# A decode kernel's key ring grows from 96 to 112 KB a partition, and neighbouring key loads share a quarter of it instead of a half

## The chip, the core and the metric

The kernel runs on one core of one Trainium2 chip. The metric is the device time of one execution in microseconds (us); the runs of the kernel before lie between 1264.14 and 1264.46 us, with a median of 1264.3. The engines are named as in the profile: PE (TensorE, with its weight loads as PEld), DVE (VectorE), ACT (ScalarE), POOL (GpSimd), SP (SyncE, which here issues nearly all DMAs). Keys and values are streamed once from HBM into SBUF, whose 128 partitions are written by 16 DMA engines.

## What is computed

One token attends to a cache of 65,536 keys and values for each of 8 key heads; two query heads share a key head. The result goes through an output projection and is mixed by a gate with a small token MLP, which is little work beside the cache.

```
B, Sq, D = 1, 1, 448
Hq, Hkv, Sk, Dh = 16, 8, 65536, 256

q = (x @ wq)                                   # 16 query heads of 256
k = jnp.repeat(k_cache, rep, axis=1)           # rep = 2
v = jnp.repeat(v_cache, rep, axis=1)
scores = jnp.einsum("bhqd,bhkd->bhqk", q, k) * (Dh ** -0.5)
p = _softmax(scores, axis=-1)
o = jnp.einsum("bhqk,bhkd->bhqd", p, v)
a = o.reshape(B, Sq, Hq * Dh) @ wo
g = _sigmoid((x * gate_w).sum(-1, keepdims=True))
return g * a + (1 - g) * b                     # b: the token MLP
```

The caches are bf16: 8 x 65,536 x 256 x 2 bytes are 268 MB each for keys and for values.

## The kernel before

**Blocks and chunks.** A *block* is 16,384 keys of one head (8 MB of keys, 8 MB of values; four blocks a head, `NP` = 32 blocks in all, numbered j = 0 to 31). Kj and Vj below are the key and the value load of block j. A partition holds 128 rows (`NV`) of 256 numbers of a block, 64 KB. A block is worked off in 8 *chunks* (`BODY`) of 16 rows (`NT`); half a block is 4 chunks (`DC`) or 64 rows (`HV`).

**The work of a block.** For each chunk PE transposes the keys (16 transposes of 128x128, L359; a pair of bf16 numbers is moved as one f32) into the four PSUM banks of `kst`; DVE (L675) and ACT (L820) copy two banks each into `ktT`, and PE multiplies them with the query (L380, 32 small matmuls), one chunk behind the transposes. After the 8 chunks DVE and PE find the running maximum (`maxima`), ACT forms the exponentials of the block (`weights`, L807, into `pT`), DVE fades the old sums, and PE adds the value products (`values`, L411, 128 matmuls). From the fourth block on the order in PE's loop is lagged: iteration j has `maxima` of block j-1, the chunks of block j, and then the values of block j-1.

**Buffers.** Values have one buffer, `vbuf`, of 64 KB a partition: Vj can be loaded when the values of block j-1 are used up (`sem_pv`). Keys have a ring, `kring`, of 192 rows or 96 KB. An even block lies in rows 0 to 127, an odd one in rows 64 to 191, so that neighbours share rows 64 to 127. Each block begins with the shared half: the chunks 0 to 3 read the ring from row 64 (`tiles(HV)`), the chunks 4 to 7 from row 0 or 128 by the parity of the block (`x2`). When a block's first 4 chunks are transposed the next block can be loaded whole. For even blocks the chunks therefore stand in another order than the rows of V, and ACT writes the two halves of the exponentials exchanged into `pT` (`pt_reg` toggles between 0 and `DC`).

**The order of the loads.** SP runs through one list, and each entry waits there until its buffer is free; nothing behind it is issued before. The list is K0 (in halves), V0, K1, V1, K2, K3, V2, K4, V3, K5, V4 and so on. The start differs from the rest: `LEAD` = 2 has K2 and K3 follow each other, K2 comes in two halves (the upper one, which is used first, with its own semaphore), and K3 in a half and two quarters, as the ring comes free; POOL waits for the two quarters and passes them on as one count of `sem_k`. The last key block comes in two halves, and the last value block in five pieces, the first of which (72 rows) goes into the key ring.

PE waits for `sem_k` before chunk 0 of each block, and before chunk 4 for `sem_kb` and, in blocks 2, 3 and 31 alone, for one of `sem_kc`.

Of the kernel before, what the change touches and what calls it, by code (L numbers as in the profile page):

```python
# [12 lines left out]
def bass_gated_mix__gqa_block_cached__mixer_token_mlp__decode_kernel(  # L13
# [14 lines left out]
    bf16 = mybir.dt.bfloat16  # L28
# [35 lines left out]
    LEAD = 2  # L64
# [18 lines left out]


    HV = NV // 2
    assert NP % 2 == 0


# [8 lines left out]
    with ctx:  # L97
        def sb(shape, dt, name):
            return ctx.enter_context(nc.sbuf_tensor(name, shape, dt))
# [4 lines left out]
        def new_sem(name):  # L104
            return ctx.enter_context(nc.semaphore(name))

        kring = sb([P, NV + HV, DH], bf16, "kring")
        kring_f = kring.bitcast(f32)
        vbuf = sb([P, NV, DH], bf16, "vbuf")
        vbuf_f = vbuf.bitcast(f32)  # L110
# [1 line left out]
        pT = sb([P, BODY, 2 * NT], bf16, "pT")  # L112
# [4 lines left out]
        ident = sb([P, P], f32, "ident")  # L117
# [72 lines left out]
        scores_all = sps[:, 0, 0:SC]  # L190
# [6 lines left out]

        sem_k = new_sem("sem_k")
        sem_kb = new_sem("sem_kb")
        sem_kc = [new_sem("sem_kc%d" % i) for i in range(3)]  # L200
        sem_kq = [new_sem("sem_kq%d" % i) for i in range(2)]
        sem_v = new_sem("sem_v")
        sem_vp = [new_sem("semvp%d" % i) for i in range(len(pieces))]
        sem_x = new_sem("sem_x")
# [5 lines left out]
        sem_tr = [new_sem("sem_tr%d" % b) for b in range(NB)]  # L210
# [46 lines left out]
        @block.sync  # L257
        def _(eng):
            def load_wo(g):
                w = A_wo[g * REP * DH:(g + 1) * REP * DH, :]  # L260
                eng.dma_start(wo_rows, w.rearrange("(p i) n -> p (i n)", i=2 * REP)).then_inc(sem_wo, 16)

            load_wo(0)
            eng.dma_start(wq_a.rearrange("p j n -> p (j n)"),
                          A_wq[0:WF * P, :].rearrange("(p j) n -> p (j n)", p=P)).then_inc(sem_wq, 16)
            eng.dma_start(wq_b, A_wq[WF * P:DM, :].rearrange("r (a n) -> (r a) n", a=2)
                          ).then_inc(sem_wq, 16)
            def load(dst, cache, j, n0, n1, at, sem):
                eng.dma_start(dst[:, at + n0:at + n1, :].rearrange("p n d -> p (n d)"), src(cache, j, n0, n1)
                              ).then_inc(sem, 16)  # L270

            load(kring, A_k_cache, 0, HV, NV, 0, sem_k)
            load(kring, A_k_cache, 0, 0, HV, 0, sem_kb)

            def load_v(j):
                if j == 0:
                    eng.wait_ge(s_q, 1)
                    eng.wait_ge(s_hb, 1)
                else:
                    eng.wait_ge(sem_pv, j)  # L280
                load(vbuf, A_v_cache, j, 0, NV, 0, sem_v)
                g, m = divmod(j, PPH)
                if m == 0 and 1 <= g < H - 1:
                    eng.wait_ge(s_proj, g)
                    load_wo(g)

            for j in range(NP):
                if j == LEAD + 1:
                    eng.wait_ge(sem_tr[NB - 1], BODY * LEAD)
                    load(kring, A_k_cache, j, HV, NV, HV, sem_kc[1])  # L290
                    eng.wait_ge(sem_tr[NB - 1], BODY * LEAD + DC // 2)
                    load(kring, A_k_cache, j, 0, HV // 2, HV, sem_kq[0])
                if j >= 1:
                    eng.wait_ge(sem_tr[NB - 1], BODY * (j - 1) + DC)
                if j == LEAD:
                    load(kring, A_k_cache, j, HV, NV, 0, sem_k)
                    load(kring, A_k_cache, j, 0, HV, 0, sem_kc[0])
                elif j == LEAD + 1:
                    load(kring, A_k_cache, j, HV // 2, HV, HV, sem_kq[1])
                elif j == NP - 1:  # L300
                    load(kring, A_k_cache, j, 0, HV, HV, sem_k)
                    load(kring, A_k_cache, j, HV, NV, HV, sem_kc[2])
                elif j >= 1:
                    load(kring, A_k_cache, j, 0, NV, HV * (j % 2), sem_k)
                if j < LEAD:
                    load_v(j)
                elif j > LEAD:
                    load_v(j - 1)


            for (n0, n1), sem in zip(pieces, sem_vp):
                if n0 == 0:
                    eng.wait_ge(sem_tr[NB - 1], BODY * (NP - 1) + DC)
                elif n0 == NRING:
                    eng.wait_ge(sem_pv, NP - 1)
                load(kring if n1 <= NRING else vbuf, A_v_cache, NP - 1, n0, n1, 0, sem)
            eng.wait_ge(s_proj, H - 1)
            for h in range(REP):
                w = A_wo[(HQ - REP + h) * DH:(HQ - REP + h + 1) * DH, :]
                eng.dma_start(wo_sb[:, h, :], w.rearrange("(p j) n -> p (j n)", j=2)).then_inc(sem_wl[h], 16)  # L320
            eng.wait_ge(s_fin, NCG)
            eng.dma_start(out_ap, out_row[:, :]).then_inc(sem_out, 16)
            eng.wait_ge(sem_out, 16)

        @block.gpsimd
        def _(eng):
            eng.memset(ident[:, :], 0.0)
            eng.drain()
            eng.affine_select(
                out=ident[:, :], in_=ident[:, :], compare_op=ALU.not_equal, fill=1.0,  # L330
                base=0, pattern=[[-1, P]], channel_multiplier=1,
            )
            eng.drain()
            eng.memset(ones_sq[:, :], 1.0).then_inc(sem_ident, 1)
            for sem in sem_kq:
                eng.wait_ge(sem, 16)
            eng.sem_inc(sem_k, 16)

        @block.tensor
        def _(pe):  # L340
# [3 lines left out]
            def transposes(k, c, j, u16, x2):  # L344
                if k == 0:
                    pe.wait_ge(sem_k, u16)
                if k == DC:
                    pe.wait_ge(sem_kb, 16)
                    for p, sem in zip((LEAD, LEAD + 1, NP - 1), sem_kc):
                        with pe.If(j == p):  # L350
                            pe.wait_ge(sem, 16)

                done = pe.snap(c + 1, min_val=1, max_val=NC)

                def tiles(at):
                    for b in range(NB):
                        pe.wait_ge(sem_ev[b], done)
                        for i in range(4):
                            ins = pe.transpose(kst[:, b, i * P:(i + 1) * P],  # L359
                                               kring_f[:, at + NT * (k % DC) + 4 * b + i, :], ident[:, :])  # L360
                        ins.then_inc(sem_tr[b], 1)

                if k < DC:
                    tiles(HV)
                else:
                    with pe.If(x2 == 0):
                        tiles(0)
                    with pe.Else():
                        tiles(NV)

            def scores(k, c, j1):
                par = k % 2
# [165 lines left out]
            with nc.Fori(0, NP + 1, 1, engines=on, head_slot={pe.engine: 0}) as jj:  # L538
                j = pe.snap(jj, min_val=0, max_val=NP)
# [239 lines left out]
        def _(act):  # L779
# [13 lines left out]
            act.wait_ge(s_q, 1)  # L793
            act.activation(qrow[:, 1, :], kst[:, 1, :], AF.Copy).then_inc(s_qc, 1)

            pt_reg = act.alloc_register("pt_reg")
            act.reg_mov(pt_reg, DC)
            mix_reg = act.alloc_register("mix_reg")
            act.reg_mov(mix_reg, 1)

            def weights(j1):
                act.wait_ge(s_mneg, j1)
                act.activation(fade[:, :], mdif[:, :], AF.Exp, scale=scale).then_inc(s_fade, 1)  # L803
                for half in range(2):
                    p0 = act.snap(pt_reg, min_val=0, max_val=DC)
                    for hh in range(REP):
                        ins = act.activation(pT[:, bass.ds(p0, DC), hh:2 * NT:REP],  # L807
                                             scores_all.rearrange("p (a r n hh) -> p a hh r n", a=2, r=DC, hh=REP)[:, half, hh],
                                             AF.Exp, bias=mneg[:, hh:hh + 1], scale=scale)
                    if half == 0:  # L810
                        act.reg_sub(pt_reg, DC, pt_reg)
                ins.then_inc(sem_exp, 1)

            with nc.Fori(0, NP, 1, engines=OrderedEngineSet([act.engine])) as j:
# [44 lines left out]
```

## Time and profile before

| quantity | value |
|---|---|
| median of the runs | 1264.3 us (1264.14 to 1264.46) |
| span of the profiled execution, first to last instruction | 1262.8 us |
| PE, DVE, ACT busy | 77%, 39%, 43% of the span |
| mean granted PE clock | 0.842 of full |
| read from HBM | 544.22 MB |
| the queue that carries it (q1, issued by SP) | 12098 packets, 99.8% of 16 engines' span |

The span begins with the first and ends with the last instruction of the profiled execution; the time of a run is 1.5 us longer than this span. Times in views count from the start of the span. The chain of waits is followed back from the last instruction: at each step to what released it. In a row such as `DMA kring<-in_A_k_cache_dram` the number ahead is the time from the issue to the landing, so it holds the time that the load queued behind others too. An `issue` row is time in which the engine waited for nothing that the profile shows. The PEclk column of a window is the granted clock, 1.00 being full speed.

### The profile page before, as it was taken

The numbers are of one execution on the slowest core, as the hardware profiler recorded it, in microseconds if no ns is written. First come the engines' busy times: TensorE is split into PE (matmuls) and PEld (weight loads), VectorE is DVE, ScalarE is ACT, GpSimd is POOL, SyncE is SP. The second block draws the span as 40 slices with busy tenths as digits, with TensorE's granted clock in tenths as the row PEclk, the third lists the DMA queues.
The fourth block names the chain that finished last, engine by engine and source line by source line (L and its number), as shares of the span: only waits on it lengthen the run. The fifth ranks groups of instructions, "written<-read, shape, count | busy, mean of one in ns | idle before, by whom it ended". The sixth has DMA issues, their size and how long they took to land.

```text
span 1262.8 us, 39606 instructions
## 1 busy us (share of the span) xinstructions
PE 974.4 (77%) x17019; PEld 891.1 (71%) x17019; DVE 498.3 (39%) x1126; ACT 545.7 (43%) x692; POOL 0.9 (0%) x7
## 2 busy tenths in 40 slices
PE   4768887678777797776977678886778866798787
PEld 3667876678667687666877667876668766687685
DVE  3234434344444435444354433342333432334342
ACT  2344643345433455343454334443344433445352
POOL 0000000000000000000000000000000000000000
PEclk8878888898877888788888889887798877888787
DMA  9999999999999999999999999999999999999998
GB/s 415 433 421 426 439 436 436 432 432 432 432 434 440 436 432 432 432 430 438 434 434 429 437 434 432 432 432 436 436 436 432 432 432 432 432 434 438 428 438 370
DMA packets 12197, 544.35 MB, mean 431 GB/s; under 512 B 1433, under 2 KB 1692, under 8 KB 2972
## 3 DMA queue, kind: packets, MB, share of 16 engines
q1 hardware_dynamic: 12098, 544.22, 99.8%
q8 instruction: 6, 0.10, 0.0%
q10 hardware_dynamic: 90, 0.01, 0.0%
q14 instruction: 3, 0.02, 0.0%
HBM read 544.22 MB, written 0.00 MB: 431 GB/s over the span
## 4 chain that ended last, share of the span: by engine, by line
DMA 58%; PE 37%; DVE 2%; issue 2%; DVEq 0%; SPq 0%; ACT 0%
DMA kring<-in_A_k_cache_dram 55%; PE kst L359 26%; PE sps L380 6%; PE acc L411 3%; DMA vbuf<-in_A_v_cache_dram 2%; DMA wo_sb<-in_A_wo_dram 1%; PE acc L461 0%; PE sps L399 0%; PE prj L472 0%; DVE ktT L675 0%; ACT z_b L825 0%; PE acc L404 0%; DVE accs L709 0%; PE sps L397 0%; DVE mrow L686 0%
## 5 line engine op out<-in xcount | busy, mean ns | idle before, releaser
L359 PE MATMUL kst<-ident,kring 128*128 128x128 f32 x4096 | 565.0, 299 | 181.4 <-DMA kring<-in_A_k_cache_dram 158.2
L359 PEld LDWEIGHTS kst<-ident,kring 128*128 128x128 f32 x4096 | 513.1, 156 | 190.7 <-issue 184.6
L820 ACT ACTIVATE ktT<-kst 128x1024 bf16<-128x1024 bf16 x512 | 499.9, 1021 | 337.2 <-PE kst L359 336.8
L675 DVE COPY ktT<-kst 128x1024 bf16<-128x1024 bf16 x512 | 353.9, 692 | 435.5 <-PE kst L359 409.4
L380 PEld LDWEIGHTS sps<-qcur,ktT 128*128 128x128 bf16 x8192 | 238.0, 97 | 2.6
L380 PE MATMUL sps<-qcur,ktT 128*128 128x2 bf16 x8192 | 236.6, 163 | 0.0
L411 PE MATMUL acc<-vbuf,pT 128*2 128x256 bf16 x4008 | 164.1, 341 | 4.6 <-issue 3.3
L411 PEld LDWEIGHTS acc<-vbuf,pT 128*2 128x2 bf16 x4008 | 113.5, 103 | 47.0 <-issue 4.5
L803 ACT ACTIVATE fade<-mdif 128x2 f32<-128x2 f32 x32 | 6.5, 203 | 305.1 <-DVE mdif L692 305.1
L686 DVE TENSOR_REDUCE mrow<-sps 2x1 f32<-2x128 f32 x32 | 8.9, 279 | 162.6 <-PE sps L397 162.6
L399 PEld LDWEIGHTS sps<-mdiag,mones 2*128 2x128 f32 x64 | 11.1, 216 | 27.9 <-DVE mdiag L688 27.9
L397 PE MATMUL sps<-ident,mcol 128*2 128x128 f32 x32 | 8.9, 279 | 27.9 <-issue 26.4
L399 PE MATMUL sps<-mdiag,mones 2*128 2x2 f32 x64 | 13.9, 284 | 21.3 <-DVE mdiag L688 21.3
L807 ACT ACTIVATE pT<-sps,mneg 128x64 f32 x128 | 30.3, 334 | 0.0
L825 ACT ACTIVATE z_b<-z_b 128x448 bf16<-128x448 bf16 x14 | 8.1, 576 | 48.2 <-DVE z_b L662 48.2
L404 PE MATMUL acc<-pT,ones_sq 128*128 128x32 bf16 x256 | 12.0, 182 | 21.9 <-issue 18.4
L397 PEld LDWEIGHTS sps<-ident,mcol 128*2 128x2 f32 x32 | 2.6, 80 | 36.6 <-issue 28.3
L709 DVE COPY accs<-acc 128x288 f32<-128x288 f32 x8 | 3.7, 458 | 61.7 <-PE acc L411 61.7
L681 DVE TENSOR_REDUCE mcol<-sps 128x2 f32<-128x256 f32 x32 | 13.5, 423 | 34.6 <-PE sps L380 34.6
L404 PEld LDWEIGHTS acc<-pT,ones_sq 128*128 128x128 bf16 x256 | 8.8, 99 | 26.0 <-issue 22.4
L704 DVE TENSOR_SCALAR acc<-acc,fader 128x256 f32<-128x256 f32 x32 | 15.8, 493 | 2.5
L691 DVE TENSOR_SCALAR mneg<-sps 128x2 f32<-128x2 f32 x32 | 5.1, 160 | 16.8 <-PE sps L399 16.8
(113 smaller groups left out, 168.8 us busy)
## 6 DMA issues: line engine op xcount, KB each, us to landing
kring<-in_A_k_cache_dram SPq DMA_DIRECT2D x7, 4096.0 KB, 25.2
kring<-in_A_v_cache_dram SPq DMA_DIRECT2D x1, 4608.0 KB, 25.4
kring<-in_A_k_cache_dram SPq DMA_DIRECT2D x2, 2048.0 KB, 13.1
wo_sb<-in_A_wo_dram SPq DMA_DIRECT2D x7, 448.0 KB, 25.3
vbuf<-in_A_wq_dram SPq DMA_DIRECT2D x1, 3072.0 KB, 10.8
vbuf<-in_A_v_cache_dram SPq DMA_DIRECT2D x1, 1536.0 KB, 8.1
vbuf<-in_A_v_cache_dram SPq DMA_DIRECT2D x1, 1024.0 KB, 10.2
vbuf<-in_A_v_cache_dram SPq DMA_DIRECT2D x1, 768.0 KB, 11.6
```

Source lines behind the costliest of these rows:

```text
L359: ins = pe.transpose(kst[:, b, i * P:(i + 1) * P], kring_f[:, at + NT * (k % DC) + 4 * b + i, :], ident[:, :])
L380: ins = pe.matmul(sps[:, 0, 2 * (NT * k + nt):2 * (NT * k + nt) + 2], ktT[:, par, b, ntl * DH + dj:(ntl + 1) * DH:2], qcur[:, dj, :], star ...
L397: pe.transpose(mxT, mcol[:, :], ident[:, :]).then_inc(s_mT, 1)
L399: pe.matmul(mxB, mones[:, :], mdiag[:, :], start=True, stop=True).then_inc(s_mB, 1)
L404: pe.matmul(acc[:, DENC:SELC], ones_sq[:, :], pT[:, r, :], start=False, stop=(r == BODY - 1), skip_group_check=True)
L411: ins = pe.matmul(acc[o:o + REP, 0:DH], pT[:, r, 2 * nt:2 * nt + 2], buf[:, n, :], start=False, stop=False, skip_group_check=True)
L675: vec.tensor_copy(ktT[:, k % KTB, b, :], kst_b[:, b, :]).then_inc(sem_ev[b], 1)
L681: vec.tensor_reduce(out=mcol[:, :], in_=scores_all.rearrange("p (n hh) -> p hh n", hh=REP), axis=AX.X, op=ALU.max)
L686: vec.tensor_reduce(out=mrow[:, :], in_=mxT, axis=AX.X, op=ALU.max)
L704: vec.tensor_scalar(acc[:, 0:DENC], acc[:, 0:DENC], fader[:, :], None, op0=ALU.mult).then_inc(s_acc, 1)
L807: ins = act.activation(pT[:, bass.ds(p0, DC), hh:2 * NT:REP], scores_all.rearrange("p (a r n hh) -> p a hh r n", a=2, r=DC, hh=REP)[:, hal ...
L820: act.activation(ktT[:, k % KTB, b, :], kst_b[:, b, :], AF.Copy).then_inc(sem_ev[b], 1)
```

## The change

The ring gets 224 rows (112 KB a partition). An odd block now lies in rows 96 to 223 (`ODD` = 96), so that neighbours share a quarter (`QV` = 32 rows, `DQ` = 2 chunks). A block begins with the shared quarter; an even one then takes rows 64 to 95 and, at last, 0 to 63, an odd one goes straight on. With this

- the load of a block from K4 on (and K1 and K2) waits for 2 chunks of the block before, not 4;
- K2 is one load on `sem_k`, with no half of its own;
- K3 is two loads, three quarters and then the quarter that is used first; POOL has no part in it any more;
- V31's first piece waits for the end of block 30's transposes, and no longer for half of block 31;
- ACT writes three groups of exponentials (2, 2 and 4 chunks) instead of two of 4.

```diff
+    QV = NV // 4
+    ODD = NV - QV
+    DQ = DC // 2
...
-        kring = sb([P, NV + HV, DH], bf16, "kring")
+        kring = sb([P, ODD + NV, DH], bf16, "kring")
...
                 if j == LEAD + 1:
                     eng.wait_ge(sem_tr[NB - 1], BODY * LEAD)
-                    load(kring, A_k_cache, j, HV, NV, HV, sem_kc[1])
-                    eng.wait_ge(sem_tr[NB - 1], BODY * LEAD + DC // 2)
-                    load(kring, A_k_cache, j, 0, HV // 2, HV, sem_kq[0])
+                    load(kring, A_k_cache, j, QV, NV, ODD, sem_kc[0])
                 if j >= 1:
-                    eng.wait_ge(sem_tr[NB - 1], BODY * (j - 1) + DC)
-                if j == LEAD:
-                    load(kring, A_k_cache, j, HV, NV, 0, sem_k)
-                    load(kring, A_k_cache, j, 0, HV, 0, sem_kc[0])
+                    eng.wait_ge(sem_tr[NB - 1], BODY * (j - 1) + DQ)
+                if j == NP - 1:
+                    load(kring, A_k_cache, j, 0, HV, ODD, sem_k)
+                    load(kring, A_k_cache, j, HV, NV, ODD, sem_kc[1])
                 elif j == LEAD + 1:
-                    load(kring, A_k_cache, j, HV // 2, HV, HV, sem_kq[1])
-                elif j == NP - 1:
-                    load(kring, A_k_cache, j, 0, HV, HV, sem_k)
-                    load(kring, A_k_cache, j, HV, NV, HV, sem_kc[2])
+                    load(kring, A_k_cache, j, 0, QV, ODD, sem_k)
                 elif j >= 1:
-                    load(kring, A_k_cache, j, 0, NV, HV * (j % 2), sem_k)
+                    load(kring, A_k_cache, j, 0, NV, ODD * (j % 2), sem_k)
...
-                    eng.wait_ge(sem_tr[NB - 1], BODY * (NP - 1) + DC)
+                    eng.wait_ge(sem_tr[NB - 1], BODY * (NP - 1))
...
-            for sem in sem_kq:
-                eng.wait_ge(sem, 16)
-            eng.sem_inc(sem_k, 16)
...
                 if k == DC:
                     pe.wait_ge(sem_kb, 16)
-                    for p, sem in zip((LEAD, LEAD + 1, NP - 1), sem_kc):
-                        with pe.If(j == p):
-                            pe.wait_ge(sem, 16)
+                    with pe.If(j == NP - 1):
+                        pe.wait_ge(sem_kc[1], 16)
+                if k == DQ:
+                    with pe.If(j == LEAD + 1):
+                        pe.wait_ge(sem_kc[0], 16)
...
-                if k < DC:
-                    tiles(HV)
+                if k < DQ:
+                    tiles(ODD + NT * k)
                 else:
                     with pe.If(x2 == 0):
-                        tiles(0)
+                        tiles(HV + NT * (k - DQ) if k < DC else NT * (k - DC))
                     with pe.Else():
-                        tiles(NV)
+                        tiles(ODD + NT * k)
...
-                for half in range(2):
-                    p0 = act.snap(pt_reg, min_val=0, max_val=DC)
+                for (k0, k1, r0), reg in zip(groups, pt_regs):
+                    p0 = act.snap(reg, min_val=min(r0, k0), max_val=max(r0, k0))
```

The list of SP (DMA issues; shapes in elements a partition, 32768 being a whole block) from V1 to K4, before:

```order
L269 DMA vbuf<-in_A_v_cache_dram 128x32768 [waits sem_pv]
L269 DMA kring<-in_A_k_cache_dram 128x16384 [waits sem_tr3]
L269 DMA kring<-in_A_k_cache_dram 128x16384
L269 DMA kring<-in_A_k_cache_dram 128x16384 [waits sem_tr3]
L269 DMA kring<-in_A_k_cache_dram 128x8192 [waits sem_tr3] x2
L269 DMA vbuf<-in_A_v_cache_dram 128x32768 [waits sem_pv]
L269 DMA kring<-in_A_k_cache_dram 128x32768 [waits sem_tr3]
```

The same stretch of the changed kernel:

```order
L272 DMA vbuf<-in_A_v_cache_dram 128x32768 [waits sem_pv]
L272 DMA kring<-in_A_k_cache_dram 128x32768 [waits sem_tr3]
L272 DMA kring<-in_A_k_cache_dram 128x24576 [waits sem_tr3]
L272 DMA kring<-in_A_k_cache_dram 128x8192 [waits sem_tr3]
L272 DMA vbuf<-in_A_v_cache_dram 128x32768 [waits sem_pv]
L272 DMA kring<-in_A_k_cache_dram 128x32768 [waits sem_tr3]
```

K2's two halves have become one load, and K3's three parts two; V2 stands behind them as before.

On PE, in front of the transposes of chunk 4 of a block, before:

```order
L380 MATMUL sps<-qcur,ktT 128x2 x32
L350 COMPARE_AND_BRANCH [waits sem_kb]
L350 UNCONDITIONAL_BRANCH [waits sem_kc0]
L350 COMPARE_AND_BRANCH
L350 UNCONDITIONAL_BRANCH [waits sem_kc1]
L350 COMPARE_AND_BRANCH
L350 UNCONDITIONAL_BRANCH [waits sem_kc2]
L366 COMPARE_AND_BRANCH
L357 REGISTER_ALU
```

And in front of the transposes of chunk 2, in the changed kernel:

```order
L377 MATMUL sps<-qcur,ktT 128x2 x31
L347 COMPARE_AND_BRANCH
L347 UNCONDITIONAL_BRANCH [waits sem_kc0]
L363 COMPARE_AND_BRANCH
L354 REGISTER_ALU
L356 MATMUL kst<-ident,kring 128x128 [waits sem_ev0]
```

The test for K3 and the test for the ring's half have moved to chunk 2, where before no test stood; chunk 4 keeps the test for block 31 and the one for the half, and the wait of block 2 for a second half is gone.

On ACT, the exponentials of a block, before and then after:

```order
L803 ACTIVATE fade<-mdif 128x2 [waits s_mneg]
L805 ISA
L807 ACTIVATE pT<-sps,mneg 128x64
L807 ISA
L807 ACTIVATE pT<-sps,mneg 128x64
L811 ISA
L807 ACTIVATE pT<-sps,mneg 128x64
L807 ISA
L807 ACTIVATE pT<-sps,mneg 128x64
```

```order
L805 ISA
L807 ACTIVATE pT<-sps,mneg 128x32
L807 ISA
L807 ACTIVATE pT<-sps,mneg 128x32
L810 ISA
L807 ACTIVATE pT<-sps,mneg 128x32
L807 ISA
L807 ACTIVATE pT<-sps,mneg 128x32
L810 ISA
L807 ACTIVATE pT<-sps,mneg 128x64
L807 ISA
L807 ACTIVATE pT<-sps,mneg 128x64
```

Four activations of 64 numbers a partition have become four of 32 and two of 64.

More of the change, by code (lines that the diff above doesn't have):

```diff
@@ L85, in bass_gated_mix__gqa_block_cached__mixer_token_mlp__decode_kernel @@
     HV = NV // 2
+    QV = NV // 4
+    ODD = NV - QV
+    DQ = DC // 2
+    assert DQ * NT == QV
     assert NP % 2 == 0
@@ L199, in bass_gated_mix__gqa_block_cached__mixer_token_mlp__decode_kernel @@
         sem_kb = new_sem("sem_kb")
-        sem_kc = [new_sem("sem_kc%d" % i) for i in range(3)]
-        sem_kq = [new_sem("sem_kq%d" % i) for i in range(2)]
+        sem_kc = [new_sem("sem_kc%d" % i) for i in range(2)]
         sem_v = new_sem("sem_v")
@@ L359, in tiles @@
                             ins = pe.transpose(kst[:, b, i * P:(i + 1) * P],
-                                               kring_f[:, at + NT * (k % DC) + 4 * b + i, :], ident[:, :])
+                                               kring_f[:, at + 4 * b + i, :], ident[:, :])
                         ins.then_inc(sem_tr[b], 1)
-                if k < DC:
-                    tiles(HV)
+                if k < DQ:
+                    tiles(ODD + NT * k)
                 else:
                     with pe.If(x2 == 0):
-                        tiles(0)
+                        tiles(HV + NT * (k - DQ) if k < DC else NT * (k - DC))
                     with pe.Else():
-                        tiles(NV)
+                        tiles(ODD + NT * k)
             def scores(k, c, j1):
@@ L794, in _ @@
             act.activation(qrow[:, 1, :], kst[:, 1, :], AF.Copy).then_inc(s_qc, 1)
-            pt_reg = act.alloc_register("pt_reg")
-            act.reg_mov(pt_reg, DC)
+            groups = [(0, DQ, BODY - DQ), (DQ, DC, DC), (DC, BODY, 0)]
+            pt_regs = []
+            for k0, k1, r0 in groups:
+                pt_regs.append(act.alloc_register("pt_reg%d" % k0))
+                act.reg_mov(pt_regs[-1], r0)
             mix_reg = act.alloc_register("mix_reg")
@@ L803, in weights @@
                 act.activation(fade[:, :], mdif[:, :], AF.Exp, scale=scale).then_inc(s_fade, 1)
-                for half in range(2):
-                    p0 = act.snap(pt_reg, min_val=0, max_val=DC)
+                for (k0, k1, r0), reg in zip(groups, pt_regs):
+                    p0 = act.snap(reg, min_val=min(r0, k0), max_val=max(r0, k0))
                     for hh in range(REP):
-                        ins = act.activation(pT[:, bass.ds(p0, DC), hh:2 * NT:REP],
-                                             scores_all.rearrange("p (a r n hh) -> p a hh r n", a=2, r=DC, hh=REP)[:, half, hh],
+                        ins = act.activation(pT[:, bass.ds(p0, k1 - k0), hh:2 * NT:REP],
+                                             scores_all.rearrange("p (r n hh) -> p hh r n", r=BODY, hh=REP)[:, hh, k0:k1],
                                              AF.Exp, bias=mneg[:, hh:hh + 1], scale=scale)
-                    if half == 0:
-                        act.reg_sub(pt_reg, DC, pt_reg)
+                    act.reg_sub(reg, r0 + k0, reg)
                 ins.then_inc(sem_exp, 1)
```

## Prediction

> **What bounds the kernel now.** I read the page first, then the chain of waits, then SyncE's own timeline.
>
> ```profile
> PE 974.4 (77%) x17019; PEld 891.1 (71%) x17019; DVE 498.3 (39%) x1126; ACT 545.7 (43%) x692; POOL 0.9 (0%) x7
> DMA  9999999999999999999999999999999999999998
> HBM read 544.22 MB, written 0.00 MB: 431 GB/s over the span
> ```
>
> The DMA row is the one to look at: its 16 engines are full in 39 of 40 slices, while the busiest compute engine, TensorE, rests 23% of the time. Does the stream ever pause? The chain of waits gives an issue time and the time to landing for each key load:
>
> ```profile
> 259.11 27.43 DMA kring<-in_A_k_cache_dram
> 286.67 5.41 PE kst L359 x32
> ...
> 453.68 27.43 DMA kring<-in_A_k_cache_dram
> ```
>
> These two, K7 and K12, land at 286.54 and 481.11. Between lie five pairs of a key and a value load (16.78 MB each pair) and one projection load of 0.46 MB, 84.35 MB in 194.57 us: 433.5 GB/s, 38.70 us a pair, 19.35 a load. The other key loads of that chain land on the same beat, so in the middle the stream has one rate and nothing that an engine does shows in it. At 433.5 GB/s all bytes take 1255.4 of the span's 1262.8 us; the rest lies at the two ends.
>
> The time can change in three ways only: the ends, the rate, or a **gap**, a moment when SyncE (SP) has no load in the queue. SP issues in program order, K(j+1) when enough of Kj is transposed and then V(j) when the values before it are used up. Its timeline shows how early:
>
> ```profile
> 84.33 0.81 SPq L269 DMA_DIRECT2D kring<-in_A_k_cache_dram  x2
> 95.69 0.33 SPq L269 DMA_DIRECT2D kring<-in_A_k_cache_dram  x1
> 112.52 5.50 SPq L269 DMA_DIRECT2D kring<-in_A_k_cache_dram  x2
> 118.07 0.43 SPq L269 DMA_DIRECT2D vbuf<-in_A_v_cache_dram  x1
> 145.76 0.33 SPq L269 DMA_DIRECT2D kring<-in_A_k_cache_dram  x1
> 165.09 0.33 SPq L269 DMA_DIRECT2D vbuf<-in_A_v_cache_dram  x1
> 180.62 0.33 SPq L269 DMA_DIRECT2D kring<-in_A_k_cache_dram  x1
> ```
>
> In order: K2 in two halves (the second at 84.70), K3's half and two quarters, V2, K4, V3, K5. Asked for the landing of K2's second half alone, and of V3, the view of DMA issues answers:
>
> ```profile
> kring<-in_A_k_cache_dram SPq DMA_DIRECT2D x1, 4096.0 KB, 26.5
> ...
> vbuf<-in_A_v_cache_dram SPq DMA_DIRECT2D x1, 23.6
> ```
>
> They landed at 111.2 and 188.7. V3 is the tight place: 23.6 us from issue to landing, against 27.4 later on, for a transfer that itself needs 19.35. K4 (23.60, below) is as tight.
>
> **The change part by part.**
>
> *Earlier key loads.* From K4 on, a key load waits for 2 transposed chunks instead of 4, so it is issued two chunks sooner. Beyond the opening this buys nothing: the load only queues longer, since the stream ahead of it has no hole. Cost and gain 0; it would be worth something only if a key load were late, and the tightest, K4, is not.
>
> *K2 whole.* This is the term that matters. TensorE now starts K2 when all of it has landed, not half:
>
> ```profile
> 101.59 5.67 PE acc L411 x121
> 107.26 1.40 issue
> 108.66 3.84 PE kst L359 x32
> ...
> 145.76 23.60 DMA kring<-in_A_k_cache_dram
> ```
>
> Before, it finished V1's values at 107.26 and began K2 at 108.66. After, it waits for 111.2 - 0.1 (the 0.1 is worked out below): **+2.5 us** (2.3 to 2.6). The idle stretch grows from 1.4 to 3.9 us, and the granted clock answers to that:
>
> ```profile
> 108.60:112.50 3.90, 3.84 (x32) 3.44 (x32) 1.00 1.02 437
> 133.90:140.60 6.70, 6.63 (x32) 6.39 (x32) 0.55 0.99 430
> 169.40:175.50 6.10, 5.93 (x32) 5.70 (x32) 0.62 0.99 430
> ```
>
> These are the first 32 transposes of K2, K3 and K4, with the clock in the fifth column (behind time, TensorE and weight loads). K2's ran at 1.00 after a short pause; the others, after longer ones, began at half clock. So K2's first 32 will cost about 5.8 instead of 3.84: **+2.0** (0 if the clock holds, 2.8 if it is low throughout as in K3). K3's 6.63 was the worst of these rows; behind another pause it should come near the others, 5.9: **-0.7** (0 to -1.2, the latter by K7's 5.41 above). The rest of K2 and K3 repeats unchanged.
>
> *Branches.* Three tests at chunk 4 become one at chunk 2 and one at chunk 4, and chunks 2 and 3 now test for the ring's half, as the later chunks did. In front of K2's chunk 4 TensorE stood so:
>
> ```profile
> 119.03 1.96 PE L359 MATMUL kst<-ident,kring 128*128 128x128 f32 x16 [0.59 <-issue]
> ```
>
> 0.59 us for four tests. Spread over three chunks, five tests come to about the same: **0** (between all of it hidden, -0.6, and 0.15 us for each test, +0.2).
>
> *V3 late.* The sum is 2.5 + 2.0 - 0.7 = **+3.8 us** (0.8 to 5.8 with all ends at once). V2's values, whose end releases V3, are behind all of it, so V3 is issued at 165.1 + 3.8 = 168.9. K5 is queued behind it on SP, but has 19 us.
>
> *Fewer small packets.* K2's second half landed at 111.2 and its first at 84.33 + 17.1 = 101.4:
>
> ```profile
> kring<-in_A_k_cache_dram SPq DMA_DIRECT2D x1, 4096.0 KB, 17.1
> ```
>
> 9.8 us for a half, where half a whole load is 9.7. I take 0.1 us for K2 and 0.1 for K3: **-0.2** (-0.4 to 0). By this K4 ends at 169.2.
>
> *Does that tear the stream?* Unbroken, V3 lands at 188.7 - 0.2 = 188.5. Issued at 168.9, it lands no sooner than 168.9 + 19.35 + D, where D is the time from issue to the first packet and from the last one to the semaphore. D is at most 23.60 - 19.35 = 4.25, since K4 and V3 kept up with that. At the other end stands the first load of all; and one row shows packets at the moment when K4's turn came (slices of 0.05 us, a digit where a packet starts):
>
> ```profile
> 0.74 0.40 SPq L261 DMA_DIRECT2D wo_sb<-in_A_wo_dram  x1
> ...
> DMA  0000000000000000000009878394019638997795
> ...
> DMA  0009000000000990990900909090000090000000
> ```
>
> The first digits are the window 0.7 to 2.7: work begins 1.0 us after the issue at 0.74, so D is at least 1.0. The second are 147 to 149: after 147.2 no packet starts until 147.65, which is 1.9 us behind K4's issue at 145.76; I read this as engines that had finished V2 and waited for K4. With some tenths for the semaphore, as an estimate between the two ends, D = 2.4. Then V3 lands at 190.65, **2.2 us late** (0.8 with D = 1.0, 4.0 with 4.25), and everything behind it is as late, because no later load has room to catch up: the stream has one rate.
>
> The Trainium skill, "DMA: Bandwidth & Descriptors", section "Latency and other measured facts", gives about 600 ns to the first byte of a DMA issued from SP; the 1.0 and 1.9 us above are both longer, so the trace decides. By that figure D would be near 1.0 and the sum +0.6 instead of +2.0.
>
> *ScalarE.* The weights of a block go from four exponentials of 128x64 to four of 128x32 and two of 128x64:
>
> ```profile
> L807 ACT ACTIVATE pT<-sps,mneg 128x64 f32 x128 | 30.3, 334 | 0.0
> L803 ACT ACTIVATE fade<-mdif 128x2 f32<-128x2 f32 x32 | 6.5, 203 | 305.1 <-DVE mdif L692 305.1
> ```
>
> Between 128x2 at 203 ns and 128x64 at 334, four of 128x32 cost at most 1.34 and at least 0.81 us, where two of 128x64 cost 0.67: 0.1 to 0.7 us more a block. Behind a load that is 19 us long this is covered; if the cover went, 32 blocks would pay 3 to 22 us. In the last block there is no later load, but there:
>
> ```profile
> 1248.97 0.95 ACT L807 ACTIVATE pT<-sps,mneg 128x64 f32 x4
> ...
> 1252.30 0.39 PE L404 MATMUL acc<-pT,ones_sq 128*128 128x32 bf16 x8 [0.63 <-issue]
> ```
>
> The weights are done at 1249.92 and used at 1252.30. **0.**
>
> *The end.* V31 comes in five pieces; the first no longer waits for half of K31:
>
> ```profile
> 1212.90 27.25 DMA vbuf<-in_A_v_cache_dram
> ...
> 1225.62 0.33 SPq L269 DMA_DIRECT2D kring<-in_A_v_cache_dram  x1
> ...
> kring<-in_A_v_cache_dram SPq DMA_DIRECT2D x1, 4608.0 KB, 25.4
> ```
>
> V30 lands at 1240.15, the piece at 1251.0: 10.9 us for 4.72 MB, which is the stream's rate. Issued at 1213.3 it lands no sooner. **0.**
>
> **Sum** against the profiled execution: 1262.8 + 2.2 - 0.2 = 1264.8. The median of the runs, 1264.3, is 1.5 above that span; so 1264.3 + 2.0 = **1266.3**. A measurement of this kernel tells apart about 0.2%, 2.5 us: by size this is no change, near the border.
>
> **The rivals.**
>
> *No gap.* If the clock holds through the pause (2.5 - 0.7 = 1.8), V3 is issued at 166.9 and lands at 188.65: 0.15 late, 0.2 won. 1264.2. For it: K2's row above has full clock right behind V1's values. Against: K3 and K4 began at half clock.
>
> *Slower.* The same mechanism at a higher price: K2's 32 transposes at half clock throughout (+2.8), K3's no better than before (0), so V3 comes at 170.4 and lands 3.7 late: +3.5, 1267.8. It decides from a V3 issued later than 169.4 (gap above 2.7). For it: K3's own row; nothing in the rows ties the clock's steps to the start of a block. Against: both blocks must be hit.
>
> *Short D.* With D = 1.0 the gap is 0.8: 1264.9. Against it: the row at 147.65. The figure of the Trainium skill quoted above, from "DMA: Bandwidth & Descriptors", is on its side.
>
> *Faster.* That earlier key loads raise the rate. For it: 431 GB/s over the span against 433.5 in the middle, 7.4 us. Against: these lie before K0's landing and behind the last piece, which the change does not touch; each load of the middle lands on the 38.70 beat. If a quarter of them were won: 1262.4; for 0.2% it would take a third, 1261.8. The Trainium skill, "DMA: Bandwidth & Descriptors", section "Where 436 GB/s comes from", puts the ceiling at 435 GB/s, by which, as an estimate, all bytes need 1251 us; the 433.5 above is just below it. That the change does not do what it says is the same case seen from SP: K(j+1) goes out sooner, and waits in the queue.
>
> **How the numbers follow.** Forecast (a gap of 1 to 2.7 us) 46%; slower 33%; no gap 10%; short D 8%; faster 3%. Within 0.2% are the forecast, no gap and short D: 0.64; slower 0.33; faster 0.03. The range goes from a little below no gap, 1263.9, to a little above the slower rival, 1268.2; outside are the faster case and the last of the slower one.
>
> **What would show it.** K2's first transposes at about 111.2 and not 108.7; 5.4 to 6.6 us for 32 of them; V3 issued at 167 to 170.5; a fall of the DMA share around 168 to 171; K4 landing at 169.2 but V3 at 190 or later; from there each landing late by the same amount and the pairs still 38.70 apart. I am wrong if V3 is issued before 166.7, if V3 lands at 188.5 in spite of a late issue, or if the 38.70 changes.

## The result, and the profile after

The changed kernel takes **1266.3 us** (median of 21 runs, 1265.03 to 1267.84) against 1264.36 of the kernel before beside it (21 runs, 1264.14 to 1265.43). The ratio is 1.0015, with a 95% interval of 1.0009 to 1.0021: 1.9 us slower, which is more than noise and less than 0.2%. The profiled execution spans 1265.7 us, 2.9 more than the one of before. A profiled execution is one of the runs: this one took 1266.98 us, 1.3 more than its span. The same 1.3 us on the span of before, 1262.8, give 1264.1, the fastest of its runs; the 1.5 us named ahead set a median against the span of another execution. The page of the changed kernel, in the three lines that were shown of the other:

```profile
PE 970.7 (77%) x17019; PEld 893.0 (71%) x17019; DVE 498.3 (39%) x1126; ACT 556.2 (44%) x756; POOL 0.9 (0%) x7
DMA  9999999999999999999999999999999999999998
HBM read 544.22 MB, written 0.00 MB: 430 GB/s over the span
```

Little is to be seen here, and that is a reading in itself: the bytes and the instructions of TensorE are the same, ScalarE is busy 10.5 us more, and a loss of 2 us is lost in a slice of 32. SyncE's timeline shows where to look (issue time, then what is loaded; K2 and K3 are the first row, then V2, K4, V3, K5, V4):

```profile
78.43 38.49 SPq L272 DMA_DIRECT2D kring<-in_A_k_cache_dram  x3
116.96 0.43 SPq L272 DMA_DIRECT2D vbuf<-in_A_v_cache_dram  x1
143.33 0.33 SPq L272 DMA_DIRECT2D kring<-in_A_k_cache_dram  x1
167.31 0.33 SPq L272 DMA_DIRECT2D vbuf<-in_A_v_cache_dram  x1
174.89 0.33 SPq L272 DMA_DIRECT2D kring<-in_A_k_cache_dram  x1
198.45 0.33 SPq L272 DMA_DIRECT2D vbuf<-in_A_v_cache_dram  x1
```

K4 goes out at 143.33 instead of 145.76 and K5 at 174.89 instead of 180.62: the key loads are sooner, as the change intends. V3 goes out at 167.31 instead of 165.09. The chain of waits says why, and what K5 did with its lead:

```profile
78.43 32.71 DMA kring<-in_A_k_cache_dram
111.26 5.30 PE kst L356 x32
...
137.58 5.72 PE kst L356 x32
...
174.89 35.85 DMA kring<-in_A_k_cache_dram
...
256.22 33.00 DMA kring<-in_A_k_cache_dram
...
450.79 33.01 DMA kring<-in_A_k_cache_dram
```

TensorE begins K2 when the whole of it has landed, at 111.1, and not at 108.66. K5 was issued 5.7 us sooner and landed at 210.74. Before, K5 was issued at 180.62 and landed 27.4 us later, at 208.1. So it is 2.7 us late in spite of its lead: 35.85 us from issue to landing, and 33.0 for later loads against 27.4, is the longer queue, no gain. K7 and K12 (the last two rows) land at 289.22 and 483.80, 194.58 us apart, where they were 194.57 apart before: the rate of the stream has not changed, only its place. What happened lies between K4 and V3. V3 in the view of DMA issues:

```profile
vbuf<-in_A_v_cache_dram SPq DMA_DIRECT2D x1, 24.1
```

Issued at 167.31, it landed at 191.4. K4 landed at 143.33 + 25.9 = 169.2, so that 188.6 would have been the beat: 2.8 us are lost at this one place, and the end is 2.9 later.

### The profile page after: what moved, and what is told of

It reads as the page before. It is cut to its first block, busy times and chain, and to the rows that moved or that the text cites. A ratio compares the mean times of both kernels' runs of the same rounds, so it can differ in the third digit from the quotient of the medians.

```text
span 1265.7 us, 39892 instructions
## 1 busy us (share of the span) xinstructions
PE 970.7 (77%) x17019; PEld 893.0 (71%) x17019; DVE 498.3 (39%) x1126; ACT 556.2 (44%) x756; POOL 0.9 (0%) x7
## 4 chain that ended last, share of the span: by engine, by line
DMA 76%; PE 22%; issue 1%; DVE 1%; SPq 0%; DVEq 0%; ACT 0%
DMA kring<-in_A_k_cache_dram 72%; PE kst L356 18%; DMA vbuf<-in_A_v_cache_dram 2%; PE sps L377 2%; PE acc L408 2%; DMA wo_sb<-in_A_wo_dram 1%; SPq L272 0%; PE acc L458 0%; PE sps L396 0%; DVE ktT L672 0%; PE prj L469 0%; PE acc L401 0%; PE sps L394 0%; DVE mrow L683 0%; DVE mdiag L685 0%
## 5 line engine op out<-in xcount | busy, mean ns | idle before, releaser
L356 PEld LDWEIGHTS kst<-ident,kring 128*128 128x128 f32 x4096 | 516.7, 156 | 191.5 <-issue 184.3
L408 PE MATMUL acc<-vbuf,pT 128*2 128x256 bf16 x4008 | 157.6, 332 | 6.0 <-issue 3.3
L408 PEld LDWEIGHTS acc<-vbuf,pT 128*2 128x2 bf16 x4008 | 110.6, 101 | 44.6 <-issue 4.9
L807 ACT ACTIVATE pT<-sps,mneg 128x32 f32 (+1 forms) x192 | 40.1, 309 | 0.1
```

The source lines that it names most:

```text
L356: ins = pe.transpose(kst[:, b, i * P:(i + 1) * P], kring_f[:, at + 4 * b + i, :], ident[:, :])
L408: ins = pe.matmul(acc[o:o + REP, 0:DH], pT[:, r, 2 * nt:2 * nt + 2], buf[:, n, :], start=False, stop=False, skip_group_check=True)
L807: ins = act.activation(pT[:, bass.ds(p0, k1 - k0), hh:2 * NT:REP], scores_all.rearrange("p (r n hh) -> p hh r n", r=BODY, hh=REP)[:, hh, k ...
```

## The experiments

Times below are medians of the runs, with the ratio to the kernel before, which ran beside each. "Issued" and "landed" are V3's, from the profiled execution.

### K2 in halves again (the changed kernel, one thing undone)

```diff
+                elif j == LEAD:
+                    load(kring, A_k_cache, j, HV, NV, 0, sem_k)
+                    load(kring, A_k_cache, j, 0, HV, 0, sem_kc[2])
...
                 if k == DC:
+                    with pe.If(j == LEAD):
+                        pe.wait_ge(sem_kc[2], 16)
```

> The changed kernel with one thing undone: K2 comes in two halves again, the half that is used first ahead. Theory (the whole loss is K2's wait, which makes V3 late and tears the stream once): TensorE starts K2 at about 108, V3 is issued at 164 to 166, lands at 188.5 to 189, time 1264.2 (1264.0 to 1264.8), as before. Rival (the larger ring, the branches or the six exponentials cost it): time stays at 1266 or more.

Measured: 1264.26 us, ratio 1.000 (0.9991 to 1.0009). K4 and V3 in SyncE's timeline of this kernel, and V3's time to landing:

```profile
137.84 0.33 SPq L272 DMA_DIRECT2D kring<-in_A_k_cache_dram  x1
162.13 0.33 SPq L272 DMA_DIRECT2D vbuf<-in_A_v_cache_dram  x1
...
vbuf<-in_A_v_cache_dram SPq DMA_DIRECT2D x1, 26.5
```

V3 lands at 188.6, on the beat, and the loss is gone. It is issued 3 us sooner than before the change, and sooner than the 164 to 166 that were expected, mostly because TensorE began K2 at 106.38 and not at about 108. The 112 KB ring, the smaller overlap, the branches and the six exponentials together cost nothing that can be measured, and bring nothing either.

### K2 whole alone (the kernel before, one thing done)

```diff
-                    load(kring, A_k_cache, j, HV, NV, 0, sem_k)
-                    load(kring, A_k_cache, j, 0, HV, 0, sem_kc[0])
+                    load(kring, A_k_cache, j, 0, NV, 0, sem_k)
```

and the wait of block 2 for `sem_kc[0]` left out.

> The kernel before with this part of the change alone: K2 as one load; ring of 96 KB, half overlap, K3 in three parts. Theory: TensorE starts K2 at 111.2, V3 is issued 2 to 4 us later than 165.1, time 1266.3 (1265.3 to 1267.3). Here K4 is also issued late (it waits for 4 chunks of K3, so at some 148 instead of 145.8) and can tear the stream a second time, so it may come out above the changed kernel, up to 1268.5. Rival (the loss is in the other parts): 1264.4.

Measured: 1266.22 us (1265.34 to 1268.36), ratio 1.0015 (1.0006 to 1.0024). V2, K4 and V3 of this kernel, and their times to landing:

```profile
123.56 0.43 SPq L269 DMA_DIRECT2D vbuf<-in_A_v_cache_dram  x1
150.70 0.33 SPq L269 DMA_DIRECT2D kring<-in_A_k_cache_dram  x1
169.56 0.33 SPq L269 DMA_DIRECT2D vbuf<-in_A_v_cache_dram  x1
...
vbuf<-in_A_v_cache_dram SPq DMA_DIRECT2D x1, 28.5
...
kring<-in_A_k_cache_dram SPq DMA_DIRECT2D x1, 21.9
...
vbuf<-in_A_v_cache_dram SPq DMA_DIRECT2D x1, 22.3
```

The loss is as large in the ring of before, but lies in two other places. The first is K3's two quarters, which wait for K2's second and fourth chunk: they were issued at 118.02 and 123.19, and the first landed 1.6 us behind the beat, the second another 0.4. V2, queued behind them, was issued at 123.56 and landed at 152.0, where it landed at 149.9 in the changed kernel (issued 116.96, 33.0 us to landing): 2.1 us late. K4, which waits here for 4 chunks of K3, was issued at 150.70 and landed at 172.6, 20.5 behind V2 where a load takes 19.35: 1.2 more. V3 then lands 19.3 behind K4, on the beat, though it was issued only 3.0 us ahead of K4's landing. In the changed kernel V2 and K4 land on time, since both go out sooner (K3's last quarter after two chunks of K2, K4 after two of K3), and the gap comes one load later, at V3. So the smaller overlap does close two gaps, where K2 is whole, and the time is the same, since V3's takes their place.

### The clock: work for TensorE while it waits for K2

```diff
+                with pe.If(j == LEAD):
+                    for _ in range(44):
+                        pe.transpose(sps[:, 1, 384:512], ident[:, :], ident[:, :])
                 with pe.If(j > LEAD):
                     maxima(pe.snap(j, min_val=1, max_val=NP))
```

> The changed kernel, with 44 transposes of the identity into an unused corner of PSUM (some 5 us at full clock) on TensorE between V1's values and K2, in the time in which it waits for K2 anyway. Theory with the clock term: K2's first 32 transposes take 3.8 to 4.5 us instead of 5.3, V3 comes 1 to 1.5 us sooner than the 167.3 of the changed kernel, and the time falls by 0.7 to 1.5 us, to 1265.0. Rival (the clock plays no part, the wait alone makes the loss): no change, 1266.3.

Measured: 1265.86 us, ratio 1.001 (1.0001 to 1.002). K2's first 32 transposes took 3.78 us, but the idle work ended at 112.5, over a microsecond after K2 had landed, so that little was won: V3 was issued at 167.70. The trial did not tell the two apart, and was made again with 30.

> As the trial with 44 transposes of the identity, but with 30, which end before K2 lands (some 3.4 us of the 4 to 5 us of waiting), so that K2 itself starts at 111.3. Theory with the clock term: K2's first 32 take 3.8 to 4.5 us, K3 starts 1 to 1.5 us sooner than the 137.5 of the changed kernel, V3 is issued at 165.5 to 166.8, the time falls below the 1265.9 of the trial with 44, to 1264.8 to 1265.4. Rival (the clock's phase at K3 gives back what K2 wins): 1265.8 or more.

Measured: 1265.57 us (1264.34 to 1266.49), ratio 1.0008 (0.9999 to 1.0017). TensorE's timeline at the start of K2 and of K3 of this kernel:

```profile
111.79 3.83 PE L356 MATMUL kst<-ident,kring 128*128 128x128 f32 x32 [1.62 <-DMA kring<-in_A_k_cache_dram]
...
136.84 5.95 PE L356 MATMUL kst<-ident,kring 128*128 128x128 f32 x32
```

In the changed kernel they took 5.30 and 5.79. Its view of windows gives the clock of these two stretches; behind the window stand its length, the busy time of matmuls and of weight loads, the granted clock, the DMA share and GB/s:

```profile
111.20:116.70 5.50, 5.30 (x32) 5.02 (x32) 0.70 0.99 429
137.50:143.40 5.90, 5.79 (x32) 5.55 (x32) 0.63 0.97 422
```

At a clock of 0.70 the 32 transposes of K2 took 1.5 us more than the 3.83 here. So the clock term is there, and V3 at 166.80 instead of 167.31 although K2 landed 0.5 us later here. K3 began 0.7 us sooner, not the 1 to 1.5 that were expected, and the time lies between the two forecasts, above 1265.4 and below 1265.8. Between the medians it is 0.7 us, with intervals that overlap: what the clock costs in the time is not shown.

### V3 late by idle work ahead of V2's values (the kernel before)

```diff
+                with pe.If(j == LEAD + 1):
+                    for _ in range(N):                 # N = 8, 20, 40
+                        pe.transpose(sps[:, 1, 384:512], ident[:, :], ident[:, :])
                 with pe.If(j != LEAD):
                     values(j, pe.snap(v_reg, min_val=1, max_val=NP))
```

> The kernel before, with 8 idle transposes (0.9 us at full clock, 1.6 at half) on TensorE ahead of V2's values, so that V3 is issued at about 166.2. By the price on record (V3 lands no sooner than issue + 21.75) nothing is lost: 188.7, 1264.4. By the changed kernel's trace, where V3 landed 24.1 us behind its issue once the queue had run empty: up to 190.3, 1265.9.

> The same with 20 idle transposes (2.3 to 4 us): V3 issued at 167.4 to 169. On record's price: lands at 189.2 to 190.8, time 1264.9 to 1266.5. With 24.1 us behind the issue: 191.5 to 193.1, time 1267.1 to 1268.7.

> The same with 40 idle transposes (4.5 to 8 us): V3 issued at 169.6 to 173. On record's price: lands at issue + 21.75, so 2.7 to 6 us late, time 1267 to 1270.5. With 24.1: 5 to 8.4 us late, 1269.4 to 1272.8. In both the loss grows by 1 us for each us of the issue; if a late V3 could be made up later in the stream it would grow by less.

Measured: 1264.60, 1266.37 and 1266.92 us; the ratios, 1.0029 (0.9996 to 1.0062), 1.004 (1.0009 to 1.007) and 1.0043 (1.0012 to 1.0075), are wide, because two of the ten runs of each kernel lay near 1280 us, which was not followed up. In the profiled executions of 8 and 20, V3 was issued at 164.86 and 164.68, no later than before, and landed on the beat: the idle work of 8 took 1.1 us, but TensorE had reached it a microsecond sooner than before, and behind 20 the values ran at full clock, 3.7 us instead of 5.3. These two profiles tell nothing on the price. With 40, V3 was issued at 168.71:

```profile
vbuf<-in_A_v_cache_dram SPq DMA_DIRECT2D x1, 22.2
```

It landed at 190.9, 2.2 us late. That is near the price on record (issue + 21.75), not 24.1. The issue came sooner than the 169.6 to 173 that were expected, and the time, 1266.92, lies just below the range that went with them.

### V3 held back behind K4 (the kernel before)

```diff
                     eng.wait_ge(sem_pv, j)
+                if j == LEAD + 1:
+                    eng.wait_ge(sem_tr[NB - 1], BODY * (LEAD + 2) + 1)
                 load(vbuf, A_v_cache, j, 0, NV, 0, sem_v)
```

> The kernel before, but V3 is held back until the first chunk of K4 is transposed (some 3 us behind K4's landing at 169.4, so V3 is issued at 172 to 174 into a queue that has run empty). By issue + 21.75 it lands at 194 to 196, 5 to 7 us late; time 1269.5 to 1271.5, the whole delay to the end. If one of the 16 engines regularly starts 2 us behind the others, as in the changed kernel's trace (24.1), 2 us more. If the stream can make up lost time, less than 1268.

Measured: 1271.42 us (1270.5 to 1271.61), ratio 1.0055 (1.004 to 1.0071): 6.9 us slower. V3 was issued at 173.41 and landed

```profile
vbuf<-in_A_v_cache_dram SPq DMA_DIRECT2D x1, 21.8
```

later, at 195.2, 6.3 us behind the beat, and the span is 1269.9, 7.1 more than that of before. A gap is carried to the end in full; the stream makes up none of it.

### The changed kernel again, twice

> The changed kernel once more, for a second profiled execution. If a late engine is the rule, V3 lands 24 us behind its issue; if it was chance, 21.7 to 22.3 us, as in the trials so far. V3 issued between 166.5 and 169.5.

> The same kernel, a third profiled execution. The same expectation: V3 issued between 166.5 and 169.5, landing 21.7 to 22.3 us later if the late engine was chance, 24 if it is the rule.

Measured: spans of 1265.8 and 1265.3 us. V3 was issued at 167.22 and at 168.28. Its time to landing, by the view of DMA issues, in the first:

```profile
vbuf<-in_A_v_cache_dram SPq DMA_DIRECT2D x1, 24.3
```

and in the second:

```profile
vbuf<-in_A_v_cache_dram SPq DMA_DIRECT2D x1, 21.8
```

So it landed at 191.5 and at 190.1: the V3 that was issued 1.1 us later landed 1.4 us *sooner*. The starts of packets show the difference. In the two rows below each digit is an eighth of a microsecond, and the window begins where V3 was issued. First the changed kernel's first profile, from 167.3 to 172.3:

```profile
DMA  0000000999990000000000000900000099990900
```

Then the second repetition, from 168.3 to 173.3:

```profile
DMA  0000000999990900000000000000000099999000
```

In both, the first packets start 0.9 to 1.0 us behind the issue, and the second packets follow 3.1 us after the first, not the 2.4 that a packet of this size takes in mid-stream (64 KB at a sixteenth of 433.5 GB/s). In the first row one engine starts alone, at 170.4, 2 us behind the others, and the load is complete only with it.

By how far ahead of K4's landing V3 was issued, most of these kernels fall into two kinds. Issued 1.9 to 3.0 us ahead of it (this kernel's first profile, its first repetition, and 30 idle transposes ahead of K2), it took 23.9 to 24.3 us. Issued 1.8 us ahead, or later (the second repetition, 44 idle transposes ahead of K2, 40 ahead of V2's values, and the trial behind K4), it took 21.8 to 22.2. In the kernel before, 4.3 us ahead, it landed on the beat. But this measure fails once: in the kernel before with K2 whole, V3 was issued 3.0 us ahead, and landed on the beat as well.

The packets tell more. A load ends with 16 packets of 4 bytes, one for each engine; in the changed kernel's first profile those of K4 lie between 166.8 and 168.8. The rows below count the packets that start between a moment ahead of K4's first end and 0.95 us behind V3's issue, when a free engine can start on V3; those under 512 B stand for engines that have ended K4. First the changed kernel's first profile (166.30 to 168.26), then the second repetition (166.30 to 169.23), then the kernel before with K2 whole (169.60 to 170.51):

```profile
DMA packets 8, 0.07 MB, mean 33 GB/s; under 512 B 7, under 2 KB 7, under 8 KB 7
DMA packets 21, 0.33 MB, mean 112 GB/s; under 512 B 16, under 2 KB 16, under 8 KB 16
DMA packets 2, 0.13 MB, mean 144 GB/s; under 512 B 0, under 2 KB 0, under 8 KB 0
```

So 7, 16 and none of the engines had run out of work. In the last kernel K4, itself late, ended on all engines within 0.6 us. The same count orders all the profiles: with no engine run out V3 landed on the beat, with 12 or 16 it took 21.8 to 22.2 us, and with 7 to 9 it took 23.9 to 24.3. In these last three one engine began V3 last, at 170.45, 170.38 and 169.87. In the first profile fifteen engines ended V3 by 188.9 and the last one at 191.1: 2.2 of the 2.8 us are those of one engine. What holds it back the trace does not tell.

### K1 and K2 in halves (the changed kernel)

```diff
+                elif j == 1:
+                    load(kring, A_k_cache, j, 0, HV, ODD, sem_k)
+                    load(kring, A_k_cache, j, HV, NV, ODD, sem_kc[3])
+                elif j == LEAD:
+                    load(kring, A_k_cache, j, HV, NV, 0, sem_k)
+                    load(kring, A_k_cache, j, 0, HV, 0, sem_kc[2])
```

> The changed kernel with K1 and K2 in two halves each, so that TensorE starts K1 and K2 when their first halves have landed (about 62.8 and 101.5). Theory: TensorE is then some 6 us ahead when it reaches V2's values, V3 is issued at 156 to 160 with a full queue, nothing is torn in any run, and the time is the floor of the stream: 1264.1, with the highest run below 1264.8. Rival (something else in the changed kernel costs time): 1265 or more. If the engines' spread at the start shrank too, up to 1 us less.

Measured: 1264.39 us (1264.18 to 1265.10), ratio 1.0001 (0.9992 to 1.001). It is the time of before again, but V3 was issued at 162.65, no sooner than with K2 in halves alone, and K2 was begun at 106.38, as there. The expectation of 156 to 160 was wrong. TensorE at the start of K1 in this kernel, and in the kernel before:

```profile
63.38 3.15 PE L418 MATMUL acc<-vbuf,pT 128*2 128x256 bf16 x56 [2.11 <-issue]
71.43 5.78 PE L366 MATMUL kst<-ident,kring 128*128 128x128 f32 x32 [4.90 <-issue]
```

```profile
72.51 6.62 PE L359 MATMUL kst<-ident,kring 128*128 128x128 f32 x32 [9.53 <-DMA kring<-in_A_k_cache_dram]
```

The wait for K1 to land is gone, but TensorE is with V0's values until 66.5 and then stands for 4.90 us in which nothing that the profile shows holds it, so that K1 begins only 1.1 us sooner. In these 4.90 us the trace has one packet of 16 KB on the queue q8, whose kind is given as instruction, from 66.74 to 67.76, and TensorE's next instruction, a register operation, starts at 69.3. The pause of 2.11 us inside V0's values has such a packet too, which ends at 61.65. That TensorE waits there for its code is likely, not shown. No kernel of the study is measurably faster than the one before.

## Why the prediction was right

The number on record, 1266.3 us, is the median that was measured, and its mechanism is the one that the runs show: K2 whole, V3 late, one gap, carried to the end. That the number agrees to a tenth is luck: V3 was issued 0.6 to 1.7 us sooner than forecast, and by the forecast's own price that would have left a gap of 0.5 us in the first profile, where 2.8 were lost. By its steps:

- **Earlier key loads buy nothing.** Right: K5 was issued 5.7 us sooner and queued longer, and the kernel with all of the change but the whole K2 stands at 1.000. Left out was what K2 whole does to the key loads: with the overlap of before, K3's quarters and K4 came 2.0 and 1.2 us late by it, and it is the smaller overlap that kept them on the beat.
- **K2 begins at 111.2.** Right: 111.26. The pause ahead of it was 5.41 us, not 3.9, since V1's values were done at 105.86 and not at 107.26.
- **The clock.** K2's first 32 transposes were put at 5.8 us and took 5.30, 5.19 and 5.79 in the three profiles; K3's, put at 5.9, took 5.79, 5.74 and 6.07. Right in kind, and 0.5 too much for the first, which twice lay below the 5.4 that were named as a sign.
- **Branches: 0.** Too small a gain. From the start of K2 to the start of K3 without K2's first 32 transposes it was 133.93 - 108.66 - 3.84 = 21.4 us before and 137.51 - 111.26 - 5.30 = 20.95 after: 0.5 us a block, twice on the way to V3 (24.5 and 24.0 from the start of K3 to V3's issue without K3's first 32). The wait of 0.59 in front of chunk 4 is gone, and in front of chunk 2 there is at most one of 0.15. One block stayed within the bound on record; that it counts twice was left out.
- **V3 issued at 168.9.** It was 167.31, 167.22 and 168.28. The 1.6 us of the first are the two terms above, 0.5 and 1.0. The ends given for this sum, 0.8 and 5.8, come to 0.5 and 5.6 when its four terms are added.
- **D = 2.4.** The price of a load that comes too late, 19.35 + 2.4 = 21.75 us, was measured at 21.8, 21.8, 21.8, 21.9 and 22.2 in five executions. But it is made up otherwise than was thought: 0.95 us and not 1.9 to the first packet, then a first packet that takes some 0.7 us longer, and the rest between the engines' starts and from the last packet to the landing. The row at 147.65 had been read wrongly as the latency: no engine had ended V2 before 147.5. And the price holds only where most engines have run out of work: in two of three profiles of the changed kernel V3 took 24.1 and 24.3, so that D was 4.8 and 4.9, above the upper end, 4.25, that was given for it.
- **2.2 us late.** It was 2.8, 2.8 and 1.3. In the first two, an issue that was put 1.6 us too late and an engine 2 us late, which was not foreseen, nearly cancel: they are near the forecast for reasons that are only in part those on record. In the third V3 was issued 0.6 us sooner than forecast and landed 0.6 sooner, as the price says.
- **Small packets: -0.2; ScalarE: 0; the end: 0.** From V1's landing to V2's the stream took some 0.15 us less than before in all three profiles, but K4 landed at 169.25, 169.33 and 169.45, since the start of the stream differs by tenths between executions. The exponentials take more time, 40.1 us in all by the row below against 30.3, and no load noticed. The first piece of V31, issued at 1215.07 instead of 1225.62, landed with the rest.

```profile
L807 ACT ACTIVATE pT<-sps,mneg 128x32 f32 (+1 forms) x192 | 40.1, 309 | 0.1
```

Of the rivals, *slower* is the nearest: a gap of 2.8 us, its size, is what two of the three profiles show, by another cause than the one named for it. *No gap* is what some runs may be: the fastest, 1265.03, has 0.7 us of it. *Short D* came from a right reading of the 1.0 us in the first load, which the trial rows confirm as the time to the first packet, though not as the whole of D. *Faster* found nothing for it.

The profiled executions lose 2.5 to 2.9 us in span, the runs 1.9 in the median and between 0.7 and 3.5. These agree: the profiled executions took 1266.98, 1267.09 and 1266.62 us and are from the upper half of the runs. That the runs scatter more than before (2.8 us between lowest and highest, against 1.3) fits a gap whose size hangs on the clock's steps and on how many engines have run out when V3's packets come; shown it is not.

## What to carry to other kernels

In a kernel whose DMA is full, the view of busy time will not show a loss of 0.2%; look in the queue's own timeline for the load with the least time between issue and landing above its own transfer, and follow who releases it. Coarsening a load (one instead of two halves) is not free when the engine that waits for it also, two blocks on, releases the load with the least slack. More room for a load that is never late changes only how long it queues. And a load is late not when the one before it has landed, but when the first engine has run out of it: here an issue 3.0 us ahead of that landing was enough where the engines ended within 0.6 us, and not where they ended 2.5 us apart.

## What was not expected of the hardware

- A load that was issued too late for the stream did not land the sooner, the sooner it was issued: 23.9 to 24.3 us behind its issue in three executions (issued 166.80, 167.22 and 167.31, when 7 to 9 of the 16 engines had run out of work), 21.8 in one of the same kernel that was issued at 168.28, when all had. 19.35 is the time of a load in mid-stream. In the three, one engine began last and ended 0.9 to 2.2 us behind the others; why is open.
- The first packet of each engine in such a load takes some 3.1 us instead of 2.4.
- The loss at the end can be more than the gap: 1.3 us at V3 and 2.5 in the span in the third profile of the changed kernel, 6.3 and 7.1 with V3 held back, but 2.8 and 2.9 in the first. The landings show where most of the rest comes from: in the third profile K7, V6, K8 and V7 each land another 0.1 to 0.2 us late and K31 0.4, with V3 held back V29 0.6. With 8 idle transposes, where nothing was torn, V29 is 0.2 late too, so these need no gap; their cause is open.
